# Attention with a top-score cut and a routed expert layer on one core: constant loads later and in fewer pieces, q's lower copy by GpSimd for pairs 2 to 9, and a new order table

## The chip, the cores and the metric

The kernel runs on one core of one Trainium2 chip. The metric is the device time of one execution in microseconds (us), lower is better. The core has TensorE (PE; PEld is its weight load), VectorE (DVE), ScalarE (ACT), GpSimd (POOL) and SyncE (SP), which here only issues transfers. Each engine works through its own instructions strictly in the order in which they stand in the program.

## The reference, cut to what matters

```python
# q, k, v: (8, 8, 576, 64) float32; tau = 0.02
scores = scale * np.matmul(q, k.transpose(0, 1, 3, 2))
thresh = np.max(scores, axis=-1, keepdims=True) - tau
scores = np.where(scores >= thresh, scores, -1000000000.0)
attn = softmax(scores)                       # over the last axis
x = heads joined of np.matmul(attn, v)       # (4608, 512)
# routed experts: 8 experts, 512 -> 1024 -> 512
logits = x @ w_gate + modality_bias[modality_id]
e_idx = np.argmax(logits, axis=1)            # one expert per token
out[token] = gate_w * (np.maximum(x @ w1[e], 0.0) @ w2[e])
```

## The kernel before

**Attention.** The 64 heads are taken in 32 pairs (4 pairs make a batch), and each pair in 9 steps of 128 query rows, 288 steps in all. A step is: scores on PE (`qk`, L819, into one of two PSUM tiles `s`), the row maximum on DVE (L828), a small addition on DVE (L830), the exponential on ACT (L834), the cut and the row sum on DVE (L846), four transposes on PE (L872), a copy on ACT (L875). The product with v (L753) follows by pairs in a tiling of PE of its own.

**Getting k and q ready.** fp32 accuracy is kept by splitting each value in a high and a low part (fp32r). For pairs 1 to 8, `load_rows` reads k and q into the single buffer `kq` in six pieces (two heads of k, two of q, one rest of each), `turn_rows` transposes it on PE (L684 a head, L690 the rests), `stack` makes the parts on POOL (L719, L721) in `q2`, k's in the lower 64 partitions and q's in the upper. Two transfers bring k's parts to `km`, and then one transfer, `move(q2[0:D], q2[D:P], 2.6)`, brings q's parts to the lower partitions too, over k's. `both_heads` builds `nk` and `qb` for the ninth step (L741 on POOL).

**Experts.** After each batch the tokens are routed (`gate`, `route`: small DVE operations, L1001 to L1034), and expert work on the tokens known so far (gathers, L1182 transposes, L1234 and L1266 matmuls) is laid between attention steps from about step 60 on. What is left runs after the attention.

**Constants.** `late_constants` loads the gate weights (`wgbd`), the modality bias and the modality numbers of all tokens (into an `xg` buffer, 8 bytes a token), computes `bias_t` on DVE, and fills the token table `tab` with one store. `bias_t` and `wgbd` are first used by the routing of batch 0.

**What sets the order.** Every operation is recorded with a due time (`at`, `tm`). `Plan.order` plays the operations through with fixed costs and takes, on each engine, the ready operation that is due first; `Plan.fill` puts matmuls on zeros (L1430) where PE would have a gap in that play. A table (`SHIFTS`) adds a small shift to due times before this. Nearly all transfers go out on SP's one queue, by `load` (L482), so a line says little and the tiles say much.

Of the kernel before, what the change touches and what calls it, by code (L numbers as in the profile page):

```python
# [341 lines left out]
def tile_attn_moe(  # L342
# [107 lines left out]
    RPOOL = 54  # L450

# [160 lines left out]
    def late_constants():  # L612
# [15 lines left out]
        mid_i = bi.t[:, 0:2 * B * NT].bitcast(I32).rearrange("p (b t two) -> p b t two", b=B, t=NT)  # L628
        mid_v = mid.bitcast(I32).rearrange("(b s two) -> b s two", s=S, two=2)
        for b in range(B):  # L630
            load(mid_i[:, b, 0:NC, :], mid_v[b, 0:SA, :].rearrange("(c p) two -> p c two", c=NC), wr=[(bi, b)], us=0.4)
        load(mid_i[:, :, NC, :], mid_v[:, S - P:S, :].rearrange("b p two -> p b two"), wr=[(bi, B)], us=0.7)
# [4 lines left out]
        def f():  # L637
            nc.vector.tensor_copy(out=mid_f[:, 1, :], in_=mid_i.rearrange("p b t two -> p (b t) two")[:, :, 0])
            nc.vector.tensor_scalar(out=mid_f[:, 0, :], in0=mid_f[:, 1, :], scalar1=0.0, scalar2=None,
                                    op0=ALU.is_equal)  # L640
        op("DVE", 0.25, f, [(bi, b) for b in range(B + 1)], [bf])
# [6 lines left out]
        for b, xs_ in ((bx, [bx]), (bi, [(bi, b) for b in range(B + 1)])):  # L648
            op("POOL", 0.45, lambda b=b: nc.gpsimd.memset(b.t, 0.0), wr=xs_ + [b])
# [19 lines left out]
    def load_rows(p):  # L669
# [3 lines left out]
        for z, src in enumerate((k, q)):  # L673
            for s in range(2):
                load(m[:, :, s, z, :], src[b, 2 * j + s, 0:SA, :].rearrange("(c p) d -> p c d", c=NC), us=0.6)
            load(rest(t)[:, :, z, :], src[b, 2 * j:2 * j + 2, SA:S, :].rearrange("s r d -> r s d"), us=0.2)
# [19 lines left out]
    def load_v(p):  # L696
        b, j = p // NPAIR, p % NPAIR
        t, r = vm2[p % 2], vr2[p % 2]
        sv = v[b, 2 * j:2 * j + 2]
        for s in range(2):  # L700
            load(t[:, s], sv[s, 0:SA, :].rearrange("(c p) d -> p c d", c=NC), us=0.6)
            load(r[s * R:(s + 1) * R], sv[:, SA:S, :].rearrange("s r d -> r s d"), us=0.2)
# [13 lines left out]
    def stack(p):  # L716
# [13 lines left out]
        for x in range(2):  # L730
            move(km[x * D:(x + 1) * D], q2[0:D, x], 1.3)
        move(q2[0:D], q2[D:P], 2.6)
# [91 lines left out]
    def soft_a(n):  # L824
# [5 lines left out]
        op("DVE", 0.21, lambda: nc.vector.tensor_scalar(out=nm[:, 1, x:x + 1], in0=nm[:, 0, x:x + 1], scalar1=-1.0,  # L830
                                                        scalar2=ntau, op0=ALU.mult, op1=ALU.add),
# [531 lines left out]
    at(30, late_constants)  # L1363
# [65 lines left out]
    def idle(g, n):  # L1429
# [3 lines left out]
    SHIFTS = [  # L1433
# [180 lines left out]
```

## Time and profile before

| | before |
|---|---|
| median of 3 runs | 1003.13 us (1002.33 to 1003.89) |
| profiled execution, its time | 999.88 us |
| its span, first to last instruction | 998.1 us |
| busy share PE, DVE, ACT, POOL | 97%, 74%, 62%, 56% |
| mean granted TensorE clock | 0.996 |

Busy shares are means over stages with different limits: attention alone at first, attention and experts from about 150 us, experts alone from about 785 us. The ends of matmuls are modelled, so a busy PE is not PE at its peak.

### The profile page before, as it was taken

To read this page: it belongs to the slowest core of one execution; us is meant where nothing else is said; L and a number is where in the kernel's file an instruction comes from. 1 tells how busy PE (TensorE), PEld (TensorE's weight loads), DVE (VectorE), ACT (ScalarE), POOL (GpSimd) and SP (SyncE) were. 2 spreads that over 40 slices of the span, in tenths; PEclk is the share of its full clock that TensorE was granted. 3 is DMA by queue.
4 is the path that set the end of the run, shared out by engine and by line. 5 is a ranking of instruction groups with operands and counts; after the bars stand their busy time and mean duration, and the time that the engine had idled before them with its cause. 6 is when DMAs were issued, how large, how long until landed. Compare 5 with 4: busy or idle time off the path is not lost.

```text
span 998.1 us, 20124 instructions
## 1 busy us (share of the span) xinstructions
PE 969.2 (97%) x6527; PEld 782.4 (78%) x6527; DVE 738.6 (74%) x1802; ACT 616.6 (62%) x1256; POOL 562.8 (56%) x693
## 2 busy tenths in 40 slices
PE   7989989999999999999999999999999999999997
PEld 6667678777888877888888778877887778888886
DVE  7889878898888888888988888878886373233341
ACT  6677667777777767777677667765775213243431
POOL 5433577475557652756666564646854679933341
PEclk9999999999999999999999999999999999999999
DMA  8787798789969975789689786987662258443421
GB/s 173 132 188 176 159 191 197 157 175 192 187 121 196 208 185 101 161 183 210 159 160 238 168 179 100 211 170 165 142 178 86 66 149 265 137 125 102 121 81 40
DMA packets 291122, 158.10 MB, mean 158 GB/s; under 512 B 199038, under 2 KB 262526, under 8 KB 289088
## 3 DMA queue, kind: packets, MB, share of 16 engines
q1 hardware_dynamic: 281696, 137.28, 63.0%
q0 software_dynamic: 7200, 18.92, 6.3%
q8 instruction: 54, 0.88, 0.4%
q10 hardware_dynamic: 2112, 0.52, 0.3%
q14 instruction: 60, 0.49, 0.2%
HBM read 85.83 MB, written 19.35 MB: 105 GB/s over the span
## 4 chain that ended last, share of the span: by engine, by line
PE 85%; DVE 5%; issue 3%; DMA 3%; ACT 1%; POOL 1%; SPq 0%; DVEq 0%; POOLq 0%; ACTq 0%
PE s L819 16%; PE bk L1266 16%; PE bk L753 15%; PE bk L1234 14%; PE bk L872 11%; PE pm L1234 3%; PE pm L1266 2%; PE bk L1182 1%; PE bk L941 1%; PE bk L885 1%; DMA tab<-pay,posi 1%; PE bk L966 1%; DVE nm L828 1%; DVE pr L846 1%; ACT e L834 1%
## 5 line engine op out<-in xcount | busy, mean ns | idle before, releaser
L828 DVE TENSOR_REDUCE nm<-s 128x1 f32<-128x576 f32 x288 | 216.4, 752 | 61.9 <-PE s L819 59.4
L834 ACT ACTIVATE e<-s,nm 128x576 f32<-128x576 f32 x288 | 213.5, 745 | 64.6 <-DVE nm L828 59.3
L846 DVE SCALAR_TENSOR_TENSOR pr<-s,nm,e 128x576 f32<-128x576 f32 x288 | 231.8, 812 | 25.7 <-ACT e L834 14.2
L819 PE MATMUL s<-km,q 128*128 128x288 f32 x1024 | 189.0, 310 | 2.9 <-DVE pr L846 2.7
L875 ACT COPY ptm<-bk 128x512 f32<-128x512 f32 x256 | 147.9, 588 | 57.8 <-PE bk L872 52.0
L819 PEld LDWEIGHTS s<-km,q 128*128 128x128 f32 x1024 | 146.9, 189 | 30.1 <-DVE pr L846 12.4
L872 PE MATMUL bk<-ident,pr 128*128 128x128 f32 x1152 | 168.8, 273 | 1.0 <-ACT kqt L687 1.0
L872 PEld LDWEIGHTS bk<-ident,pr 128*128 128x128 f32 x1152 | 137.3, 140 | 19.0 <-issue 3.3
L753 PE MATMUL bk<-ptm,v_m 128*64 128x320 f32 (+1 forms) x1024 | 137.8, 412 | 0.2
L753 PEld LDWEIGHTS bk<-ptm,v_m 128*64 128x64 f32 x1024 | 68.2, 136 | 48.8 <-issue 8.3
L1234 PE MATMUL bk<-xh,w1h 128*128 128x512 f32 (+2 forms) x244 | 92.6, 379 | 0.0
L1266 PE MATMUL bk<-w2h,hh 128*128 128x512 f32 x204 | 88.0, 431 | 3.0 <-DVE hl L1248 2.8
L721 POOL TENSOR_TENSOR q<-kqt,q 128x576 fp32r<-128x576 f32 x62 | 88.2, 1423 | 4.0
L1218 POOL TENSOR_TENSOR w1l<-raw,w1h 128x512 fp32r<-128x512 f32 x64 | 82.8, 1294 | 4.4
L1234 PE MATMUL bk<-xh,w1l 128*128 128x512 f32 (+2 forms) x244 | 85.2, 349 | 0.0
L1234 PE MATMUL bk<-xl,w1h 128*128 128x512 f32 (+2 forms) x244 | 85.1, 349 | 0.0
L1218 POOL TENSOR_TENSOR w2l<-raw,w2h 128x512 fp32r<-128x512 f32 x64 | 82.0, 1283 | 4.5
L719 POOL CAST q<-kqt 128x576 fp32r<-128x576 f32 x62 | 41.1, 665 | 72.7 <-PE s L819 54.9
L1266 PE MATMUL bk<-w2h,hl 128*128 128x512 f32 x204 | 80.9, 397 | 0.0
L1266 PE MATMUL bk<-w2l,hh 128*128 128x512 f32 x204 | 80.8, 396 | 0.0
L1216 POOL CAST w1h<-raw 128x512 fp32r<-128x512 f32 x64 | 39.6, 619 | 67.0 <-PE bk L1234 58.0
L1246 ACT ACTIVATE hh<-bk 128x512 fp32r<-128x512 f32 (+3 forms) x74 | 38.6, 521 | 58.8 <-PE bk L1234 58.1
(232 smaller groups left out, 1780.3 us busy)
## 6 DMA issues: line engine op xcount, KB each, us to landing
raw<-in_moe_w_dram SPq DMA_DIRECT2D x128, 256.0 KB, 4.0
km<-q SPq DMA_DIRECT2D x60, 288.0 KB, 4.4
q<-q SPq DMA_DIRECT2D x30, 576.0 KB, 5.1
nk<-km SPq DMA_DIRECT2D x97, 144.0 KB, 3.8
traw<-in_moe_w_dram SPq DMA_DIRECT2D x48, 256.0 KB, 3.0
v_m<-in_v_dram SPq DMA_DIRECT2D x64, 128.0 KB, 3.3
xs<-xr SPq DMA_DIRECT2D x32, 256.0 KB, 3.1
kq<-in_q_dram SPq DMA_DIRECT2D x46, 144.0 KB, 3.7
```

The lines of the kernel that those rows point to most:

```text
L719: op("POOL", 0.665, lambda s=s: nc.gpsimd.tensor_copy(out=q2[:, 0, s], in_=kqt[:, s]), [kqt[:, s]], [q2[:, 0, s]])
L721: op("POOL", 1.5, lambda s=s: nc.gpsimd.tensor_tensor(out=q2[:, 1, s], in0=kqt[:, s], in1=f32(q2[:, 0, s]), op=ALU.subtract), [kqt[:, s], ...
L753: nc.tensor.matmul(out=o, lhsT=lhsT, rhs=rhs, start=start, stop=stop, skip_group_check=True)
L819: nc.tensor.matmul(out=g.t[:, hf, 0:SH], lhsT=a, rhs=x, start=(z == 0), stop=(z == len(passes) - 1))
L828: op("DVE", 0.753, lambda: nc.vector.tensor_reduce(out=nm[:, 0, x:x + 1], in_=g.t[:, :, 0:SH], axis=AX.XY, op=ALU.max, negate=True), [g], ...
L834: op("ACT", 0.747, lambda: nc.scalar.activation(out=e, in_=g.t[:, :, 0:SH], func=AF.Exp, bias=nm[:, 0, x:x + 1]), [g, nm[:, 0, x:x + 1]], ...
L846: op("DVE", 0.88, lambda: nc.vector.scalar_tensor_tensor(out=pr.rearrange("p (a x) -> p a x", a=2), in0=g.t[:, :, 0:SH], scalar=nm[:, 1, x ...
L872: op("PE", 0.44, lambda: [nc.tensor.transpose(out=g.t[:, kc * P:(kc + 1) * P], in_=pr[:, kc * P:(kc + 1) * P], identity=ident) for kc in r ...
L875: op("ACT", 0.583, lambda: nc.scalar.copy(out=o, in_=g.t.rearrange("a (k p) -> a k p", p=P)), [g], [o])
L1218: op("DVE" if d else "POOL", 0.902 if d else 1.37, lambda: (nc.vector if d else nc.gpsimd).tensor_tensor(out=lo.t, in0=raw.t, in1=f32(hi.t ...
L1234: nc.tensor.matmul(out=g.t[:, 0:WT], lhsT=a.t[:, cs], rhs=x.t[:, c, 0:WT], start=(c == 0 and y == 0), stop=(c == KC - 1 and y == 2))
L1266: nc.tensor.matmul(out=g.t, lhsT=a.t[:, ts], rhs=w.t, start=(y == 0 and i == 0), stop=(y == F2 - 1 and i == 2))
```

## The change

- `late_constants` is due at 54 in place of 30, and the modality numbers come in two loads in place of nine; each load now moves 64 partitions by 72 or 71 elements of 8 bytes.
- `load_v` reads v of pairs 1 to 8 in one transfer for both heads, each partition four neighbouring rows, and `load_rows` reads k in the same order of rows, so that the keys of the scores and the rows of v still agree.
- For pairs 2 to 9 (`p < QPOOL`; pairs 0 and 1 go by heads) the last transfer of `stack` becomes two POOL copies.
- The table of shifts is replaced by one with a shift for every operation. (`NMPOOL` is 0, so L830 stays on DVE.)

```diff
+    QPOOL = 10
...
-        for b in range(B):
-            load(mid_i[:, b, 0:NC, :], mid_v[b, 0:SA, :].rearrange("(c p) two -> p c two", c=NC), wr=[(bi, b)], us=0.4)
-        load(mid_i[:, :, NC, :], mid_v[:, S - P:S, :].rearrange("b p two -> p b two"), wr=[(bi, B)], us=0.7)
+        NM = N // R
+        mid_i = bi.t[:, 0:2 * NM].bitcast(I32).rearrange("p (m two) -> p m two", two=2)
+        mid_v = mid.bitcast(I32).rearrange("(m r two) -> r m two", r=R, two=2)
+        for h in range(2):
+            load(mid_i[h * R:(h + 1) * R, 0:NM - h, :], mid_v[:, h:, :], wr=[(bi, h)], us=1.6)
...
-                load(m[:, :, s, z, :], src[b, 2 * j + s, 0:SA, :].rearrange("(c p) d -> p c d", c=NC), us=0.6)
+                kc = src[b, 2 * j + s, 0:SA, :]
+                load(m[:, :, s, z, :], kc.rearrange("(p c) d -> p c d", c=NC) if z == 0 else
+                     kc.rearrange("(c p) d -> p c d", c=NC), us=0.6)
...
+        if 0 < p < ROWS:
+            load(t.rearrange("p s c d -> p s (c d)"), sv[:, 0:SA, :].rearrange("s (p c) d -> p s (c d)", c=NC), us=1.2)
+        else:
+            for s in range(2):
+                load(t[:, s], sv[s, 0:SA, :].rearrange("(c p) d -> p c d", c=NC), us=0.6)
...
+        if p < QPOOL:
+            for s in range(2):
+                op("POOL", 1.33, lambda s=s: nc.gpsimd.tensor_copy(out=q2[0:D, :, s], in_=f32(q2[D:P, :, s])),
+                   [q2[D:P, :, s]], [q2[0:D, :, s]])
+            return
         move(q2[0:D], q2[D:P], 2.6)
...
-    at(30, late_constants)
+    at(54, late_constants)
...
-        (515427, 173, 233, 0.3), (614633, 760, 820, 3), (985271, 408, 558, 0.1), (531926, 381, 406, 0.3),
...
+        "PrPZREQHT-OWP<OiOQPYQTP4O~PIT8N|M=Q(Q'O{N>R5OKS~KMPqPSQ$PSPMPKPSP]P<PgPUPZPWPDPIPbPlPJP?PVT9LUS|NFPb"
...
+    for o, x, y in zip(plan.ops, SHIFTS[0::2], SHIFTS[1::2]):
+        o.due = o.due + (91 * digit[x] + digit[y] - 4140) / 100
```

The first place is SP's queue where the constants stand: the modality numbers and bias go to `xg`, the gate weights to `wgbd`, the fill to `tab`; the `kq` rows below them are the load of pair 4. Before:

```order
L482 DMA xg_100<-in_moe_modality_id_dram 128x4x2
L482 DMA wgbd<-in_moe_w_gate_dram 64x4x8
L482 DMA q_162<-q_162 64x2304
L482 DMA xg_100<-in_moe_modality_id_dram 128x4x2 x6
L482 DMA xg_99<-in_moe_modality_bias_dram 128x16
L482 DMA xg_100<-in_moe_modality_id_dram 128x4x2
L482 DMA tab<-xr_192 128x592
L482 DMA xg_100<-in_moe_modality_id_dram 128x8x2
L482 DMA wgbd<-in_moe_w_gate_dram 64x4x8
L482 DMA qb_167<-q_162 64x2x64
L482 DMA kq<-in_k_dram 64x2x64
L482 DMA kq<-in_q_dram 64x2x64
```

The same place now:

```order
L484 DMA qb_167<-q_162 64x2x64
L484 DMA xg_100<-in_moe_modality_id_dram 64x71x2
L484 DMA xg_100<-in_moe_modality_id_dram 64x72x2
L484 DMA wgbd<-in_moe_w_gate_dram 64x4x8
L484 DMA kq<-in_q_dram 128x4x64
L484 DMA kq<-in_k_dram 128x4x64
L484 DMA wgbd<-in_moe_w_gate_dram 64x4x8
L484 DMA xg_99<-in_moe_modality_bias_dram 128x16
L484 DMA kq<-in_k_dram 64x2x64
L484 DMA kq<-in_q_dram 128x4x64
L484 DMA kq<-in_k_dram 128x4x64
L484 DMA kq<-in_q_dram 64x2x64
```

Twelve issues for constants and the fill of `tab` stood ahead of pair 4's load; now three stand ahead of its first piece, two more between its pieces, and `tab` is filled 17 rows further on, between pieces of pair 5's load.

The second place is PE around the ends of pairs 4 and 5's transposes (`bk<-ident,kq` 128x128: a head of the single buffer `kq`). Before, at step 25; the first of the two transposes is pair 4's last, the second pair 5's first:

```order
L819 MATMUL s_76<-km_164,q_162 128x288 x4
L872 MATMUL bk_79<-ident,pr_180 128x128 x4
L872 MATMUL bk_78<-ident,pr_179 128x128 x4
L684 MATMUL bk_77<-ident,kq 128x128 x4
L684 MATMUL bk_80<-ident,kq 128x128 x4
L819 MATMUL s_75<-km_164,q_162 128x288 x4
L872 MATMUL bk_79<-ident,pr_181 128x128 x4
L819 MATMUL s_76<-nk,qb_167 128x288 x6
```

Now, with both heads of pair 5 behind the step on `nk` (step 26):

```order
L835 MATMUL s_75<-nk,qb_167 128x288 x6
L889 MATMUL bk_78<-ident,pr_178 128x128 x4
L769 MATMUL bk_77<-ptm_0_182,v_m_171 64x256 x4
L691 MATMUL bk_80<-ident,kq 128x128 x4
L691 MATMUL bk_79<-ident,kq 128x128 x4
L835 MATMUL s_76<-km_165,q_163 128x288 x4
L697 MATMUL bk_78<-ident,kq 128x64 x2
```

Pair 4's last transpose stands 18 rows above the first of these two, with five score steps between; before, nothing stood between them.

The third place is POOL where pair 2's copy comes in (`q_162` is its `q2`; `rp<-pr` is the small copy of each step). Before, the cast for `qb` waits for the transfer that fills the lower half:

```order
L859 COPY rp<-pr_179 128x64
L859 COPY rp<-pr_180 128x64
L741 CAST qb_167<-q_162 64x2x64
L719 CAST q_163<-kqt 128x576
L721 TENSOR_TENSOR q_163<-kqt,q_163 128x576
```

Now:

```order
L876 COPY rp<-pr_181 128x64
L745 CAST q_162<-q_162 64x2x576 x2
L757 CAST qb_167<-q_162 64x2x64
L876 COPY rp<-pr_178 128x64
L876 COPY rp<-pr_179 128x64
L730 CAST q_163<-kqt 128x576
L732 TENSOR_TENSOR q_163<-kqt,q_163 128x576
```

The two copies stand between small copies of two steps, and must wait until k's parts have been read from the half that they overwrite. In the rest of the program PE holds the same real matmuls; the matmuls on zeros that `fill` adds number 145 in place of 119, and the first transposes of gathered tokens stand behind step 58 in place of step 60.

## Rows read from the trace of the kernel before

**Rows 1.** Page, part 1: engine, busy us, share of the span, instructions.
```profile
PE 969.2 (97%) x6527; PEld 782.4 (78%) x6527; DVE 738.6 (74%) x1802; ACT 616.6 (62%) x1256; POOL 562.8 (56%) x693
```
**Rows 2.** Stretches of 25 us: length, busy by engine, clock, DMA share, GB/s.
```profile
core 0: us, PE busy (x) PEld busy (x) DVE busy (x) ACT busy (x) POOL busy (x), PEclk, DMA share, GB/s
25.00:50.00 25.00, 23.82 (x176) 17.23 (x177) 21.22 (x55) 17.11 (x31) 10.09 (x23) 1.00 0.70 132
50.00:75.00 25.00, 22.14 (x178) 17.45 (x179) 21.01 (x55) 17.65 (x33) 7.80 (x19) 1.00 0.82 189
75.00:100.00 25.00, 24.24 (x187) 17.74 (x187) 22.69 (x57) 19.16 (x35) 8.03 (x20) 1.00 0.78 174
100.00:125.00 25.00, 24.12 (x204) 17.16 (x203) 21.88 (x67) 15.77 (x30) 13.65 (x23) 1.00 0.75 160
125.00:150.00 25.00, 22.45 (x179) 18.14 (x176) 19.99 (x51) 17.27 (x36) 20.02 (x25) 1.00 0.92 191
```
**Rows 3.** Line L828, one instruction a step, in two of these stretches.
```profile
50.00:75.00 25.00, 8.26 (x11) 1.00 0.82 189
75.00:100.00 25.00, 9.23 (x13) 1.00 0.78 174
```
**Rows 4.** Waits of PE, whole span: who for whom, us, times, longest.
```profile
PE bk L684 <- DMA kq<-in_q_dram: 3.9, 3, 2.5
...
PE bk L753 <- DVE oh L1009: 2.8, 4, 1.3
...
PE bk L1182 <- DMA xg<-xs,tb: 2.2, 1, 2.2
```
**Rows 5.** Chain that ended last, 0 to 135 us: start, us, what.
```profile
47.45 2.08 DMA kq<-in_q_dram
...
49.97 0.83 PE bk L1430 x13
...
61.66 2.84 DMA kq<-in_q_dram
```
**Rows 6.** Timeline of PE: start, us; idle before and releaser in brackets.
```profile
49.66 0.30 PE L690 MATMUL bk<-ident,kq 64*128 64x64 f32 x2 [0.75 <-DMA kq<-in_q_dram]
...
64.59 0.63 PE L684 MATMUL bk<-ident,kq 128*128 128x128 f32 x4 [2.53 <-DMA kq<-in_q_dram]
```
**Rows 7.** Timeline of SP's queue near the constants.
```profile
37.81 5.10 SPq L482 DMA_DIRECT2D xg<-in_moe_modality_id_dram  x6
...
46.80 0.60 SPq L482 DMA_DIRECT2D kq<-in_k_dram  x1
```
**Rows 8.** DMA, 41 to 42 us: packets; queue, packets, MB, engine share.
```profile
DMA packets 1074, 0.01 MB, mean 8 GB/s; under 512 B 1074, under 2 KB 1074, under 8 KB 1074
...
q1 hardware_dynamic: 1074, 0.01, 59.9%
```
**Rows 9.** Page, part 6: transfers, count, KB each, median us to landing.
```profile
q<-q SPq DMA_DIRECT2D x30, 576.0 KB, 5.1
```
**Rows 10.** Timeline of POOL: the cast of 64 by 576 values.
```profile
45.11 0.66 POOL L741 CAST nk<-km 64x576 fp32r<-64x576 f32 x1 [0.37 <-PE s L819]
```
**Rows 11.** Timeline, 190 to 198 us: POOL and DVE.
```profile
194.56 1.43 POOL L721 TENSOR_TENSOR q<-kqt,q 128x576 fp32r<-128x576 f32 x1
194.57 1.48 DVE L1006 SCALAR_TENSOR_TENSOR fe<-l,iota_m 128x40 f32<-128x40 f32 x1
```
**Rows 12.** Lines of DVE to 125 us: busy, mean ns, idle before.
```profile
L846 DVE SCALAR_TENSOR_TENSOR pr<-s,nm,e 128x576 f32<-128x576 f32 x51 | 41.3, 814 | 4.2 <-ACT e L834 1.8 <-POOL q L721 0.6
```
**Rows 13.** The same, 125 to 800 us.
```profile
L846 DVE SCALAR_TENSOR_TENSOR pr<-s,nm,e 128x576 f32<-128x576 f32 x238 | 191.3, 812 | 21.5 <-ACT e L834 12.4 <-PE bk L872 2.6 <-DVE nm L830 0.5
```
**Rows 14.** Line L1006, one a batch: ns min/median/max, first and last start.
```profile
L1006 DVE SCALAR_TENSOR_TENSOR fe<-l,iota_m x8: 199/582/1476, 108.1 to 782.5; 128x40 f32<-128x40 f32 x8
```
**Rows 15.** Timeline of the start.
```profile
3.27 0.51 SPq L482 DMA_DIRECT2D raw<-in_q_dram  x1
...
3.99 0.62 SPq L482 DMA_DIRECT2D y<-in_q_dram  x1
...
7.40 1.33 PE L819 MATMUL s<-km,q 128*128 128x288 f32 x8
...
23.40 0.76 DVE L828 TENSOR_REDUCE nm<-s 128x1 f32<-128x576 f32 x1
```
**Rows 16.** Lines of PE, whole span: the matmuls on zeros.
```profile
L1430 PE MATMUL bk<-zero 128*128 128x128 bf16 x119 | 8.0, 219 | 0.0
```

More of the change, by code (lines that the diff above doesn't have):

```diff
@@ L450, in tile_attn_moe @@
     RPOOL = 54
+    NMPOOL = 0
+    QPOOL = 10
     def tm(n):
@@ L627, in late_constants @@
              us=0.2)
-        mid_i = bi.t[:, 0:2 * B * NT].bitcast(I32).rearrange("p (b t two) -> p b t two", b=B, t=NT)
-        mid_v = mid.bitcast(I32).rearrange("(b s two) -> b s two", s=S, two=2)
-        for b in range(B):
-            load(mid_i[:, b, 0:NC, :], mid_v[b, 0:SA, :].rearrange("(c p) two -> p c two", c=NC), wr=[(bi, b)], us=0.4)
-        load(mid_i[:, :, NC, :], mid_v[:, S - P:S, :].rearrange("b p two -> p b two"), wr=[(bi, B)], us=0.7)
+        NM = N // R
[3 more added lines that the diff above has]
+            load(mid_i[h * R:(h + 1) * R, 0:NM - h, :], mid_v[:, h:, :], wr=[(bi, h)], us=1.6)
+        mid_b = mid_i[:, :, 0].rearrange("p (b m) -> p b m", b=B)
         mid_f = bf.t[:, 0:2 * B * NT].rearrange("p (a x) -> p a x", a=2)
@@ L637, in f @@
         def f():
-            nc.vector.tensor_copy(out=mid_f[:, 1, :], in_=mid_i.rearrange("p b t two -> p (b t) two")[:, :, 0])
+            mid_t = mid_f[:, 1, :].rearrange("p (b t) -> p b t", b=B)
+            nc.vector.tensor_copy(out=mid_t[:, :, 0:NC], in_=mid_b[:, :, 0:2 * NC:2])
+            nc.vector.tensor_copy(out=mid_t[:, :, NC], in_=mid_b[:, :, 2 * NC - 1])
             nc.vector.tensor_scalar(out=mid_f[:, 0, :], in0=mid_f[:, 1, :], scalar1=0.0, scalar2=None,
                                     op0=ALU.is_equal)
-        op("DVE", 0.25, f, [(bi, b) for b in range(B + 1)], [bf])
+        op("DVE", 0.25, f, [(bi, 0), (bi, 1)], [bf])
         for m, (t, key) in enumerate(((bias_t, bias_t), (bias_u, bu))):
@@ L647, in late_constants @@
            [bias_t, bu], [bias_t])
-        for b, xs_ in ((bx, [bx]), (bi, [(bi, b) for b in range(B + 1)])):
+        for b, xs_ in ((bx, [bx]), (bi, [(bi, 0), (bi, 1)])):
             op("POOL", 0.45, lambda b=b: nc.gpsimd.memset(b.t, 0.0), wr=xs_ + [b])
@@ L699, in load_v @@
         sv = v[b, 2 * j:2 * j + 2]
+        if 0 < p < ROWS:
[3 more added lines that the diff above has]
+                load(t[:, s], sv[s, 0:SA, :].rearrange("(c p) d -> p c d", c=NC), us=0.6)
         for s in range(2):
-            load(t[:, s], sv[s, 0:SA, :].rearrange("(c p) d -> p c d", c=NC), us=0.6)
             load(r[s * R:(s + 1) * R], sv[:, SA:S, :].rearrange("s r d -> r s d"), us=0.2)
@@ L829, in soft_a @@
                                                          negate=True), [g], [nm[:, 0, x:x + 1]], hot=1)
-        op("DVE", 0.21, lambda: nc.vector.tensor_scalar(out=nm[:, 1, x:x + 1], in0=nm[:, 0, x:x + 1], scalar1=-1.0,
-                                                        scalar2=ntau, op0=ALU.mult, op1=ALU.add),
+        pool = n < NMPOOL
+        op("POOL" if pool else "DVE", 0.21, lambda: (nc.gpsimd if pool else nc.vector).tensor_scalar(
+            out=nm[:, 1, x:x + 1], in0=nm[:, 0, x:x + 1], scalar1=-1.0, scalar2=ntau, op0=ALU.mult, op1=ALU.add),
            [nm[:, 0, x:x + 1], ntau], [nm[:, 1, x:x + 1]], hot=1)
@@ L1562, in tile_attn_moe @@
+    digit = {c: i for i, c in enumerate(c for c in map(chr, range(35, 127)) if c != chr(92))}
+    assert len(SHIFTS) == 2 * len(plan.ops)
+    for o, x, y in zip(plan.ops, SHIFTS[0::2], SHIFTS[1::2]):
+        o.due = o.due + (91 * digit[x] + digit[y] - 4140) / 100
     with tc.manual_schedule():
```

123 lines of the change are left out of this document (115 added, 8 removed), and 119 rows, old and new, of the table SHIFTS.

## The prediction

> **What bounds the kernel now.** I began with the busy shares: PE is busy 969.2 of 998.1 us [rows 1], so about 29 us of PE's idle time, and what PE does for nothing, is all that a new order can win. The table of stretches shows where: the first 150 us. There PE is idle 1.2, 2.9, 0.8, 0.9 and 2.6 us in five stretches [rows 2], while only attention runs. In that stage DVE sets the pace. It is busy 21.2 and 21.0 of 25 us in the second and third stretch and 22.7 in the fourth [rows 2], and the fourth takes 13 steps where the third takes 11 [rows 3]. So the second and third stretch hold a stall that the fourth doesn't have. PE's waits name it: `kq<-in_q_dram`, 3.9 us in three waits [rows 4]. In the chain of waits two of these stand out, a transfer at 47.45 and one at 61.66 [rows 5], and the timeline gives what PE lost to them: 0.75 us before 49.66 and 2.53 us before 64.59 [rows 6]. From 150 us on, PE has little idle time; its larger waits there are 2.8 us for `oh` of the routing and 2.2 us for one gather [rows 4].
>
> **The wait before 49.66.** It is pair 4's rest of q. SP issued its load as late as 47.45, next after k's at 46.80, because SP had been issuing constants: six of the modality loads alone took 5.10 us from 37.81 on [rows 7]. Now five issues stand where eight modality loads and the rest did, and only three of them ahead of pair 4's first piece. At 0.85 us an issue (5.10 / 6) that is some 6 us of SP's time less, more than the 2 us that the load was late by. I take the 0.75 us as gone. Behind it, 13 matmuls on zeros took 0.83 us [rows 5], put there for a gap; `fill` no longer places any at this step, so they go too: 1.6 us together.
>
> **The wait before 64.59.** Here the constants have no part. Pair 5's first transposes stood straight behind pair 4's last in PE's order, but their load, into the same buffer, was issued at 61.66 and took 2.84 us [rows 5]. The new order puts five score steps between the two, about 10 us at 25 / 11 us a step [rows 3], against a load that needs some 3 to 4 us with its issue. The fill of `tab` stands among these loads now; one issue more. I take the 2.53 us as gone.
>
> **What they are worth.** 1.6 + 2.5 = 4.1 us on PE. But DVE must use them. If the second and third stretch ran at the fourth's DVE share, they would gain (22.69 - 21.22) + (22.69 - 21.01) = 3.15 us of DVE work [rows 2], which at that share is 3.15 x 25 / 22.69 = 3.5 us. I take **-3.5 us**, with 0 and -4.1 as bounds.
>
> **The start.** SP's first two loads were head 0's; now head 1's come first, and SP's halves of head 0 are fifth and sixth, issued about where 3.27 and 3.99 stand [rows 15]: 2 us later. The first scores, at 7.40 [rows 15], would come up to 2.1 us later. In exchange head 1 is made ready ahead of the steps and not between steps 2 and 4, and the same DVE work is done either way. Counting the new DVE order forward from a first maximum at about 10.4, with two steps in about 4.1 us, I get the eighth at about 23.4, where it stands before [rows 15]. I take **0**, with 0 and +2.1 as bounds.
>
> **Experts two steps earlier.** The stage without experts loses two steps. PE is idle 5.7 of 100 us from 25 to 125 us (1.18 + 2.86 + 0.76 + 0.88) [rows 2], and two steps take about 4.2 us: 4.2 x 0.057 = **-0.2 us**, bounds 0 and -0.5.
>
> **q's lower copy on POOL.** A cast of 64 by 576 values takes 0.66 us [rows 10]; each copy holds twice that, 1.3 us, and there are 16: 21 us more for POOL between about 35 and 210 us. No row shows a POOL copy that moves values to other partitions, so below the bound is this 21 us, and above it, at L721's 1.43 us for 576 values a partition [rows 11], 16 x 2.9 = 46 us. I take the first, since a cast is nearest. Cover: POOL is busy 8 to 14 of 25 us until 125 us and 20 in the next stretch [rows 2], and the result is wanted steps later. Behind a copy stand the small copies `rp`, whose source buffer DVE needs four steps on, some 8 us; without this cover a copy would cost DVE its 1.3 us, or 4 to 5 with the landing of `km` that it waits for. In exchange eight transfers of 576 KB, 5.1 us to landing [rows 9], go from a queue whose engines are 0.70 to 0.92 busy [rows 2]. The one later DMA wait of PE that they could shorten is the gather's 2.2 us [rows 4]. I take **0**, with +5 and -2.2 as bounds.
>
> A rule speaks against these copies. At 194.57 the routing's `fe`, which reads two SBUF operands, took 1.48 us while a two-operand POOL operation ran from 194.56 to 195.99 [rows 11]; the fastest `fe` takes 199 ns, the median 582 [rows 14]. The Trainium skill (SBUF — State Buffer, Who interferes with whom) says why: VectorE and GpSimd share a port pair that is locked for a whole instruction, and a VectorE instruction with two SBUF inputs waits for GpSimd's reads, one with a single SBUF input does not. By that rule, the trace agrees, the 288 long DVE operations, which read PSUM and at most one SBUF tensor, lose nothing: `pr` takes 814 ns where POOL is mostly idle and 812 where it is busy [rows 12, 13]. The routings of batches 0 and 1 fall among the copies. One hit each would be 2 x 1.3 = 2.6 us at most; in eight routings PE lost 2.8 us by `oh` [rows 4], 0.35 each. I leave it at 0, with +2.6 as bound.
>
> **v and k loads.** One v load for two, in longer runs: PE waits nowhere for v above, so 0. Where v was hidden it stays so.
>
> **The rest of the order.** 26 more matmuls on zeros at 8.0 / 119 = 0.067 us are 1.7 us [rows 16] where no gap is under them, and nothing where one is. The waits after 150 us are drawn anew: 2.2 + 2.8 us [rows 4] could go, as much could come. I take 0, with -5 and +5 as bounds.
>
> **Sum.** -3.5 + 0 - 0.2 + 0 + 0 = -3.7 us. The profiled execution's span of 998.1 becomes 994.4, its time of 999.88 becomes 996.2. It lies 3.25 us under the median of the runs, 1003.13, and the forecast is made for that median: 1003.13 - 3.7 = **999.4 us**.
>
> **Rivals.**
> *The stall only moves.* `kq` remains one buffer, and every pair's load waits for the transposes of the pair before; the new table may put another pair where pair 5 was. For it: three such waits stand in the early trace, at different pairs [rows 4]. Against it: at both known places the distance grew. Half the gain is lost and some fills cost: about 1002.5 us.
> *Slower: the modality packets block the loads behind them.* From 41 to 42 us 1074 packets of 8 bytes kept 59.9% of 16 engines busy [rows 8], so 16 x 0.599 us / 1074 = 8.9 ns each. The old nine loads had 8 x 512 + 1,024 = 5,120 of them, spread over 9 us; the two new ones have 64 x (72 + 71) = 9,152, next to each other: 9,152 x 8.9 ns / 16 = 5.1 us of the whole DMA, directly ahead of pair 4's load on the same queue. If that load lands 5.1 us later and PE stands at its first transpose, the old 1.6 us wait grows to 5.1 and pair 5 comes late in turn: 1003.13 + 5.1 - 1.6 = 1006.6 us. It decides as soon as the slack of pair 4's load is under 5 us; I count about 4 to 5 us between its landing and step 19, so it is near.
> *More than the stall.* The copies' DMA time and the new table also take away the gather's and `oh`'s waits: 999.4 - 4 = 995.4 us.
>
> **Chances.** Forecast 0.44 (996.5 to 1001 by itself), more 0.14, moved stall 0.20, blocked loads or another mishap of the start 0.22. A measurement of this kernel can tell about 0.2%, 2 us. So faster 0.58, same 0.20, slower 0.22. The range from 994.5 to 1005 holds all but the low half of the third rival and the high half of the second.
>
> **What would show it.** Right: no PE wait for `kq` over 1 us between 25 and 75 us; 12 or 13 steps in each of these stretches; DVE near 22.5 of 25 us there; POOL copies of 1.3 us with DVE never waiting for `rp`; first scores near 9.5 and the eighth maximum near 23.4. Wrong: a wait of 2 us or more for `kq` before step 30, or POOL copies of 2 us and more; new PE waits after 150 us of over 5 us in sum.

## The result, and the profile after

| | before | after |
|---|---|---|
| median of 4 runs | 1002.73 us (1001.81 to 1003.89) | 1012.05 us (1011.22 to 1013.00) |
| profiled execution, its span | 998.1 us | 1010.2 us |
| mean granted TensorE clock | 0.996 | 0.993 |

The changed kernel is **slower**: a ratio of 1.0086, 95% interval 1.0068 to 1.0104. 999.4 us was forecast, and the range ended at 1005.0.

The page's first part, against [rows 1]: engine, busy us, share, instructions.

```profile
PE 975.1 (97%) x6553; PEld 790.3 (78%) x6553; DVE 738.4 (73%) x1803; ACT 618.1 (61%) x1256; POOL 579.4 (57%) x709
```

PE does the same work but for 26 matmuls on zeros; yet it is busy 5.9 us longer and idle 6.2 us longer (1010.2 - 975.1 against 998.1 - 969.2). The stretches of 25 us, against [rows 2], show both:

```profile
core 0: us, PE busy (x) PEld busy (x) DVE busy (x) ACT busy (x) POOL busy (x), PEclk, DMA share, GB/s
25.00:50.00 25.00, 21.48 (x165) 16.39 (x162) 20.56 (x54) 16.95 (x30) 15.13 (x27) 1.00 0.77 125
50.00:75.00 25.00, 23.73 (x159) 17.16 (x159) 18.74 (x45) 15.00 (x27) 10.20 (x21) 0.87 0.59 140
75.00:100.00 25.00, 24.23 (x184) 18.30 (x183) 22.47 (x58) 19.33 (x35) 12.12 (x23) 1.00 0.59 141
100.00:125.00 25.00, 22.59 (x201) 17.02 (x200) 23.30 (x66) 16.40 (x31) 9.78 (x18) 1.00 0.50 112
125.00:150.00 25.00, 20.97 (x165) 16.12 (x163) 17.36 (x44) 13.86 (x27) 21.77 (x31) 0.93 0.66 158
```

Idle time alone misleads here. From 50 to 75 us PE is busier than before (23.73 against 22.14) with fewer matmuls (159 against 178): the clock was 0.87 in the mean, so 0.13 x 25 = 3.3 us of PE's time were lost to it. Idle time and lost clock together are 12.0 + 3.3 + 1.8 = 17.0 us from 25 to 150 us; before, at a clock of 1.00 throughout, they were 8.2 [rows 2]. That is 8.8 us, most of the loss. From 150 to 790 us PE is hardly idle, 5.2 and 1.4 us in two long stretches, so little is left there to make it good with (same columns).

```profile
150.00:450.00 300.00, 294.78 (x2147) 240.44 (x2146) 256.46 (x644) 218.21 (x460) 179.80 (x201) 1.00 0.78 166
450.00:790.00 340.00, 338.63 (x2415) 274.67 (x2414) 277.45 (x691) 235.07 (x498) 205.65 (x228) 1.00 0.73 165
```

The row maxima, one a step, show when the loss comes. Steps are counted from 0. Step 20 stood 8.3 us later than before (61.36 for 53.05), step 50 only 4.2, step 62 9.1, and the last one 10.9; in a second profile of the changed kernel (`after_again`) these were 7.9, 5.0, 6.2 and 13.4. So the new order makes good a part of a first delay by itself, and then loses again. DVE's timelines, steps 50 and 62, first before, then after:

```profile
122.79 0.75 DVE L828 TENSOR_REDUCE nm<-s 128x1 f32<-128x576 f32 x1
149.72 0.76 DVE L828 TENSOR_REDUCE nm<-s 128x1 f32<-128x576 f32 x1
```

```profile
127.00 0.76 DVE L844 TENSOR_REDUCE nm<-s 128x1 f32<-128x576 f32 x1
158.84 0.76 DVE L844 TENSOR_REDUCE nm<-s 128x1 f32<-128x576 f32 x1 [0.55 <-PE s L835]
```

PE's waits in the whole span, against [rows 4]:

```profile
PE s L835 <- DVE pr L863: 11.4, 16, 3.4
PE pm L1199 <- DVE xl L1204: 4.9, 1, 4.9
PE bk L769 <- DVE oh L1026: 2.7, 4, 1.2
PE bk L697 <- DMA kq<-in_q_dram: 1.9, 1, 1.9
```

Two places stand behind the two slow clocks. **The first, 37 to 54 us.** SP's timeline, against [rows 7] (start, us):

```profile
37.21 3.84 SPq L484 DMA_DIRECT2D xg<-in_moe_modality_id_dram  x2
41.09 2.76 SPq L484 DMA_DIRECT2D wgbd<-in_moe_w_gate_dram  x1
43.96 0.55 SPq L484 DMA_DIRECT2D kq<-in_q_dram  x1
...
48.71 0.62 SPq L484 DMA_DIRECT2D kq<-in_q_dram  x1
```

And PE's timeline, against [rows 6] (idle before and releaser in brackets):

```profile
47.85 1.07 PE L835 MATMUL s<-nk,qb 128*128 128x288 f32 x6 [1.57 <-DVE pr L863]
48.76 0.60 PE L889 MATMUL bk<-ident,pr 128*128 128x128 f32 x4
51.27 0.44 PE L697 MATMUL bk<-ident,kq 64*128 64x64 f32 x2 [1.91 <-DMA kq<-in_q_dram]
51.64 1.33 PE L835 MATMUL s<-km,q 128*128 128x288 f32 x4
52.76 1.05 PE L889 MATMUL bk<-ident,pr 128*128 128x128 f32 x4
```

Three issues took 6.6 us. Two things came late by it. DVE stood 1.25 us for the modality numbers, and its `pr` behind that released PE's first wait:

```profile
45.31 0.19 DVE L642 CAST y<-xg 128x32 f32<-128x32 int32 x1 [1.25 <-DMA xg<-in_moe_modality_id_dram]
```

And pair 4's rest of q went out at 48.71 (before at 47.45 [rows 5]), which was PE's second wait. It is the last of the load's six pieces now; before, the rests were the first two. Behind the waits the same four transposes took 1.05 us instead of 0.60: PE had fallen from the upper clock level (2.4 GHz) to the lower (1.2 GHz). The granted clock was 0.50 from 51.0 to 56.5 us.

**The second, 118 to 134 us.** POOL's timeline:

```profile
118.07 0.98 POOL L1055 DMA_INDIRECT tab<-pay,posi  x1 [0.30 <-issue]
119.04 0.42 POOL L876 COPY rp<-pr 128x64 f32<-128x64 f32 x2
126.54 1.15 POOL L745 CAST q<-q 64x1152 fp32r<-64x1152 f32 x1 [7.08 <-DMA tab<-pay,posi]
...
130.84 0.58 POOL L876 COPY rp<-pr 128x64 f32<-128x64 f32 x3
```

DVE's and PE's timelines there:

```profile
131.46 0.82 DVE L863 SCALAR_TENSOR_TENSOR pr<-s,nm,e 128x576 f32<-128x576 f32 x1 [3.45 <-POOL rp L876]
...
132.34 1.33 PE L835 MATMUL s<-km,q 128*128 128x288 f32 x4 [3.40 <-DVE pr L863]
133.46 1.05 PE L889 MATMUL bk<-ident,pr 128*128 128x128 f32 x4
```

Pair 6's copy of q stood 7.08 us, not for k's transfers but for the scatters of the routing, which POOL had issued just before. Behind it stood two more scatters, a cast and the small copies `rp`; DVE needed their source buffer, PE needed DVE, and then the clock fell. In the built program the copy's waits say the same (`DMASW` 1 to 3 belong to the three scatters ahead of it, `DMAHW` 4 and 7 to the two transfers of k's parts, which had been issued at 112.22 and 114.50):

```
L876 COPY rp<-pr_181 128x64
L745 CAST q_162<-q_162 64x2x576 [waits DMASW3_49,DMAHW4_49,DMASW2_49,DMAHW7_49,DMASW1_49,Pool_49]
L1055 DMA tab<-pay,posi_204 37888x2 [waits Pool_49]
```

In `after_again` the copy stood 5.84 us, but DVE only 1.06, and the clock was 1.00 from 100 to 150 us. What this place costs differs between executions.

### The profile page after: what moved, and what is told of

It reads as the page before. It is cut to its first block, busy times and chain, and to the rows that moved or that the text cites. A ratio compares the mean times of both kernels' runs of the same rounds, so it can differ in the third digit from the quotient of the medians.

```text
span 1010.2 us, 20147 instructions
## 1 busy us (share of the span) xinstructions
PE 975.1 (97%) x6553; PEld 790.3 (78%) x6553; DVE 738.4 (73%) x1803; ACT 618.1 (61%) x1256; POOL 579.4 (57%) x709
## 4 chain that ended last, share of the span: by engine, by line
PE 82%; DVE 9%; issue 3%; DMA 3%; POOL 1%; ACT 1%; SPq 1%; POOLq 0%; DVEq 0%; ACTq 0%
PE s L835 16%; PE bk L1251 16%; PE bk L769 14%; PE bk L1283 14%; PE bk L889 10%; PE pm L1283 3%; PE pm L1251 2%; DVE pr L863 2%; DVE nm L844 2%; DMA tab<-pay,posi 1%; PE bk L902 1%; PE bk L958 1%; PE bk L1199 1%; PE bk L983 1%; DVE fe L1023 1%
## 5 line engine op out<-in xcount | busy, mean ns | idle before, releaser
L835 PE MATMUL s<-km,q 128*128 128x288 f32 x1024 | 191.1, 313 | 10.2 <-DVE pr L863 9.1
L769 PE MATMUL bk<-ptm,v_m 128*64 128x256 f32 (+1 forms) x1024 | 138.2, 413 | 0.8 <-ACT ptm L895 0.8
L1265 DVE SCALAR_TENSOR_TENSOR hl<-bk,hh 128x512 fp32r<-128x512 f32 (+3 forms) x78 | 46.2, 594 | 55.9 <-ACT hh L1263 55.7
L1283 PE MATMUL bk<-w2h,hh 128*128 128x512 f32 x196 | 84.1, 429 | 0.0
L1263 ACT ACTIVATE hh<-bk 128x512 fp32r<-128x512 f32 (+3 forms) x78 | 41.1, 527 | 60.2 <-PE bk L1251 59.4
L1283 PE MATMUL bk<-w2h,hl 128*128 128x512 f32 x196 | 77.5, 395 | 0.0
L1283 PE MATMUL bk<-w2l,hh 128*128 128x512 f32 x196 | 77.4, 395 | 0.0
```

The source lines that it names most:

```text
L769: nc.tensor.matmul(out=o, lhsT=lhsT, rhs=rhs, start=start, stop=stop, skip_group_check=True)
L835: nc.tensor.matmul(out=g.t[:, hf, 0:SH], lhsT=a, rhs=x, start=(z == 0), stop=(z == len(passes) - 1))
L1265: op("DVE", 0.1 + 0.58 * WT / 512, lambda: nc.vector.scalar_tensor_tensor(out=hl.t[:, 0:WT], in0=g.t[:, 0:WT], scalar=0.0, in1=f32(hh.t[:, ...
L1283: nc.tensor.matmul(out=g.t, lhsT=a.t[:, ts], rhs=w.t, start=(y == 0 and i == 0), stop=(y == F2 - 1 and i == 2))
```

## The experiments

Each ratio is to runs of the kernel before on the same chip; 0.001 is about 1 us. The runs lie on several chips, and the changed kernel itself measured 1.0086 on one and 1.0128 on another, so small differences between two ratios are not read as gains. **Theory A** at first: the loss lies at three places, the late first scores and the two above. **Rival B**: the GpSimd copies cost something at every pair. **Rival C**: the order as such.

**1. The transfer back, for all eight pairs and for two.**

```diff
-                op("POOL", 1.33, lambda s=s: nc.gpsimd.tensor_copy(out=q2[0:D, :, s], in_=f32(q2[D:P, :, s])),
+                op("POOL", 1.33, lambda s=s: nc.sync.dma_start(out=f32(q2[0:D]), in_=f32(q2[D:P])) if s else None,
```

In the second kernel this holds for `p in (6, 7)` only.

> The changed kernel in its own order, but q's lower copy of pairs 2 to 9 is again one transfer on SP, issued where the second GpSimd copy stood. Theory A (the loss lies at three places: first scores 4.3 us later, 45 to 62 us, and 119 to 132 us, where a GpSimd copy stands 7.1 us before the scatters' landing and the small copies rp behind it hold the row maxima): only the third goes, 3 to 5 us of it, so 1007 to 1009 us, and no wait of DVE for rp over 1 us is left. Rival B (the copies cost something at each of the eight pairs, by GpSimd's queue or by a port shared with DVE): 6 us or more go, 1006 us or less. Rival C (the order alone, the copies cost nothing): 1011 to 1013 us.

> The changed kernel, with the transfer back for pairs 6 and 7 alone, whose copies stand behind scatters or gathers on GpSimd's queue; the other twelve copies stay on GpSimd. Theory A: as much as with all eight pairs undone, 3 to 5 us, so 1007 to 1009 us. Rival B: only a quarter of what all eight pairs give, 1 to 2 us, so 1010 to 1011 us. Rival C: 1011 to 1013 us.

Measured: 1.0111 (1.0081 to 1.0140) and 1.0081 (1.0056 to 1.0107). Rival B is not borne out: without the copies this order is no faster. With all eight transfers back, pair 2's stands on SP among the pieces of pair 4's load, and PE's wait for pair 4's rest of q grows from 1.9 to 3.7 us. Theory A isn't borne out either: undoing the copies of pairs 6 and 7, the second place, gave nothing that can be measured here, although in its profile DVE's wait for `rp` is gone and the clock is 1.00 from 75 to 150 us.

**2. Fewer packets for the modality numbers.** First in longer runs:

```diff
-        mid_v = mid.bitcast(I32).rearrange("(m r two) -> r m two", r=R, two=2)
+        mid_w = mid.bitcast(I32).rearrange("(r m two) -> r m two", r=R, two=2)
```

> The changed kernel, but the two loads of the modality numbers read 72 neighbouring tokens for a partition (about 130 packets instead of 9,152; the same two issues and the same bytes). Each token gets another token's number, so the biases of the gate are dealt out otherwise. Theory A with the packets as the cause of the second place (k's and q's rests lie behind them in the queue): DVE's wait for them at 45 us and PE's wait for q's rest at 51 us (1.9 us) go, 1 to 3.5 us, so 1008.5 to 1011 us. Rival (the second place is the order of the issues on SP, the packets are hidden): 1011.5 to 1012.5 us.

Then in one load of 71 runs, turned by PE:

```diff
+            g = fin["spare"]()
+            nc.tensor.transpose(out=g[:, 0:71], in_=bi.t[0:71, 256:384], identity=ident[0:71, 0:71])
```

> The changed kernel in its own order, but the modality numbers come in one load of 71 runs of 1 KB (71 packets instead of 9,152), issued where the first of the two loads stood, and are turned by one transpose on PE where DVE turned them into floating point. The output is the reference's, so the routing is as in the changed kernel. Theory A (the packets hold up k's and q's rests behind them, which stops the steps at 45 to 62 us): at step 20 the row maximum stands at most 4 us behind before instead of 8.3, and 3 to 5 us of the loss of 8.6 go: a ratio to before of 1.0035 to 1.0055. Rival (the run with long runs gained in its tail by its other routing): 0 to 2 us, a ratio of 1.0065 to 1.009.

Measured: 1.0027 (1.0001 to 1.0054) and 1.0095 (1.0067 to 1.0124). The first was a false trail: it leaves out the right numbers, so its experts get other tokens and its work behind the attention isn't the same. Whether that made its time is not shown: its last row maximum stood at 772.2 us and its span ended at 1001.4, with the reference's routing in `a_pe_numbers` these were 774.4 and 1011.4, but in `after_again`, with the reference's routing too, 777.5 and 1006.1. In the second run the first place is mended in part. SP's timeline:

```profile
37.86 0.72 SPq L634 DMA_DIRECT2D xg<-in_moe_modality_id_dram  x1
38.63 0.64 SPq L484 DMA_DIRECT2D wgbd<-in_moe_w_gate_dram  x1
...
44.69 0.61 SPq L484 DMA_DIRECT2D kq<-in_q_dram  x1
```

PE's wait for the rest of q is gone and step 20's row maximum stands at 58.2 us in place of 61.4 (before 53.1), 5.1 us late where theory A wanted at most 4. Still the time did not follow, and the steps show where the gain went: at step 50 0.2 us of its 3.2 are left (126.83 for 127.00). The packets by themselves aren't the loss.

**3. The parts in the order of before.** `b_two_loads` has the two modality loads alone, `b_pool_copies` the copies alone, `b_parts` all three parts, `b_pool_pe` the copies and the numbers by PE. The copies, at the transfer's place in the order:

```diff
-        move(q2[0:D], q2[D:P], 2.6)
+        def copy():
+            for s in range(2):
+                nc.gpsimd.tensor_copy(out=q2[0:D, :, s], in_=f32(q2[D:P, :, s]))
+        op("SP", 0.62, copy if p < 10 else lambda: nc.sync.dma_start(out=f32(q2[0:D]), in_=f32(q2[D:P])),
+           [q2[D:P]], [q2[0:D]], dma=2.6)
```

> The kernel before in its own order; only the transfer of q's parts for pairs 2 to 9 is replaced, at its place in the order, by two GpSimd copies. In this order the copies of pair 6 stand ahead of the scatters and one pair's stand behind scatters and gathers. Theory A (a copy costs only where it stands behind indirect transfers or a late transfer of k): within 2 us of before, 1001 to 1005 us. Rival B (a cost at every pair, some 0.5 us or more each): 1007 us or more. A gain from q being ready earlier: below 1001 us.

> The kernel before in its own order; only its nine loads of the modality numbers (5,120 packets) are replaced by the changed kernel's two (9,152 packets), issued at the place of the second and third of the nine. Packets as the cause (4,032 more at 8.9 ns over 16 queues, 2.2 us, ahead of pair 4's load): 1 to 4 us slower, a ratio of 1.001 to 1.004, and PE's wait for pair 4's rest of q at 49.7 us grows. Rival (seven issues fewer on SP, some 4 us, let pair 4's load start earlier and outweigh the packets): a ratio of 0.997 to 0.9995.

> All three parts of the change (two loads of the numbers, one load of v and k in the new order of rows for pairs 1 to 8, GpSimd's copies for pairs 2 to 9), but in the order of the kernel before: what stays away is the new order and the later constants. If the parts lose: a ratio of 1.004 or more. If the new order loses and the parts give what the copies alone gave (0.997): 0.995 to 1.001.

> The kernel before in its own order, with GpSimd's copies for pairs 2 to 9 (alone a ratio of 0.997) and the modality numbers in one load of 71 packets with a transpose on PE instead of nine loads of 5,120 packets. If packets ahead of pair 4's load are what delays the steps at 45 to 52 us in this order too: the wait before 49.7 us goes and the ratio is 0.993 to 0.996. If they are hidden here: 0.996 to 0.998, as with the copies alone.

| | ratio | 95% |
|---|---|---|
| b_pool_copies | 0.9970 | 0.9952 to 0.9989 |
| b_two_loads | 0.9998 | 0.9977 to 1.0019 |
| b_parts | 0.9988 | 0.9971 to 1.0005 |
| b_pool_pe | 0.9955 | 0.9935 to 0.9975 |

So the parts lose nothing where the order is that of before; the copies win about 3 us (1 to 5). In `b_pool_pe` DVE is busy as the prediction wanted it from 50 to 75 us (against 21.01 before); so it is in `b_pool_copies` and `b_parts` (22.61 each), without the new order. `b_pool_copies` and `b_pool_pe` beat both kernels; which of the two is faster is not shown. `b_pool_pe`:

```profile
50.00:75.00 25.00, 23.31 (x180) 17.80 (x179) 22.57 (x59) 18.21 (x35) 10.73 (x22) 1.00 0.64 149
```

Rival C stands: what loses is the new order, the later constants with it. **Theory D**: it loses in the first 150 us, where PE's idle time and clock say so. **Rival E**: later.

**4. Where the order loses.** The changed kernel with all its parts, its operations laid out by a written list, two orders spliced at a step: one order up to that step's row maximum, the other order for all that is left.

```diff
-        for i in plan.fill(plan.order(4, marks["close"]), 4, idle):
-            o = plan.ops[i]
+        plan.order(4, marks["close"])
+        ROW = (
...
+        for x in ROW.split():
+            i, *bk = x.split(":")
...
+            o = plan.ops[int(i)]
```

> The changed kernel, unaltered, beside the three orders of the same call: a ratio to before of 1.0068 to 1.0104, as measured first.

> The changed kernel with all its parts; the order of the kernel before up to the row maximum of step 62 (some 150 us), and from there its own. Theory D (the order loses, and it loses in the first 150 us: there PE's idle time and the time lost to the lower clock together rise from 13.7 to 22 us, later they hardly differ): a ratio of 0.997 to 1.002. Rival E (the new order loses later, between steps, gathers and experts): 1.006 or more.

> The reverse: the changed kernel with its own order up to step 62, and from there the order of the kernel before. Theory D: the loss stays, a ratio of 1.006 to 1.010. Rival E: 0.997 to 1.003.

> The changed kernel with the order of the kernel before up to step 20 only (some 53 us: the first loads, the constants and pair 4's load lie in it), then its own. Theory D: the start and the place at 45 to 62 us are mended, the one at 119 to 132 us (4.7 us of PE's idle and clock by the windows) stays: a ratio of 1.003 to 1.006. If the first 53 us hold the whole loss: 0.997 to 1.002. Rival E: 1.006 or more.

> The changed kernel with the order of the kernel before up to step 8 only (some 26 us: the first loads and scores), then its own. If the late first scores cost what they show (4.3 us at the first row maximum, 3 at the eighth): 3 us less than the changed kernel, a ratio of 1.005 to 1.008. If PE makes good use of the wait (its idle time in the first 25 us is no longer than before, 4.9 against 5.4 us) and the place at 45 us decides: no gain, a ratio of 1.009 to 1.013.

> The changed kernel with the order of the kernel before up to step 40 (some 96 us). With the same up to step 20 the ratio was 1.0069, up to step 62 it was 1.0009. If what is left after step 20 is the place at 119 to 132 us: 1.005 to 1.008, as up to step 20. If it is lost between 53 and 96 us: 1.000 to 1.003.

> The changed kernel's parts with its own order up to step 20 only (some 53 us), and the order of the kernel before from there. All of the parts in the order of before had a ratio of 0.9988, all in the new order 1.0086 and 1.0128. If the first 53 us of the new order cost what taking them away gave (about half): 1.003 to 1.007. If the rest of before's order makes good for them: 0.997 to 1.002.

| | order to the step | from there | ratio | 95% |
|---|---|---|---|---|
| after_again | after | after | 1.0128 | 1.0091 to 1.0164 |
| o_a62_b | after, 62 | before | 1.0122 | 1.0077 to 1.0167 |
| o_b8_a | before, 8 | after | 1.0087 | 1.0058 to 1.0116 |
| o_b20_a | before, 20 | after | 1.0069 | 1.0046 to 1.0093 |
| o_b40_a | before, 40 | after | 1.0060 | 1.0038 to 1.0082 |
| o_b62_a | before, 62 | after | 1.0009 | 0.9991 to 1.0028 |
| o_a20_b | after, 20 | before | 1.0057 | 1.0035 to 1.0079 |

Theory D holds from both sides: with the first 62 steps in the order of before the loss is gone, with only these in the new order it is all there. Steps 0 to 20 in the new order cost 1.0057 - 0.9988 = 0.69% (0.4 to 1.0), 7 us. Steps 20 to 40 cost nothing that can be told, steps 40 to 62 cost 1.0060 - 1.0009 = 0.5% (0.2 to 0.8), 5 us. Taken away, steps 0 to 20 gave less: from 1.0086 and 1.0128 to 1.0069, 0.2 to 0.6%. The profiles agree: behind a new start the order of before leaves step 50 9.2 us late (`o_a20_b`), the new order only 4.2. The start alone (`o_b8_a`) gives nothing clear back.

**5. The copy behind the scatters, by itself.** Once taken away where the first 20 steps are mended, by the edit of experiment 1, and once put into the order of before, as here against `b_pool_copies` (long lines shortened):

```diff
             sent.append(i)
+            if len(sent) == 3:
+                held.pop()()
...
-        op("SP", 0.62, copy if p < 10 else
+        op("SP", 0.62, (lambda: held.append(copy)) if p == 6 else copy if p < 10 else
```

> As o_b20_a (order of the kernel before up to step 20, a ratio of 1.0069), and q's parts of pairs 6 and 7 by a transfer instead of GpSimd's copies, which there stand behind scatters and gathers. If DVE's wait for rp behind these copies (3.5 us) and the clock behind it are what is left: 4 to 6 us less, a ratio of 1.000 to 1.004. If it only moves (the transfer is as late): 1.005 to 1.009.

> The kernel before in its own order with GpSimd's copies for pairs 2 to 9 (alone a ratio of 0.997), and one thing moved: pair 6's two copies are issued right behind the third scatter, as in the changed kernel, where they wait for the three scatters' landing. If this wait alone costs what it shows in the changed kernel (GpSimd idle some 7 us, DVE waiting 1 to 6 us for rp, then half clock): 3 to 7 us more than with the copies in their old place, a ratio of 1.000 to 1.004. If it is harmless in this order: 0.995 to 0.999.

Taken away: 1.0049 (1.0024 to 1.0074) against 1.0069, which is no clear gain. In its profile the clock is 1.00 up to 150 us and step 62 comes where it came before (149.65), but step 80 5.2 us later (206.96 for 201.75): the delay has moved behind step 62. Put in: 1.0028 (1.0011 to 1.0044) against 0.9970, so **in the order of before this one move costs 0.58% (0.3 to 0.8), 6 us**, and its profile has the same waits as the changed kernel's. POOL's timeline, then DVE's:

```profile
111.68 0.98 POOL L1045 DMA_INDIRECT tab<-pay,posi  x1 [0.32 <-issue]
122.03 2.23 POOL L737 CAST q<-q 64x1152 fp32r<-64x1152 f32 x2 [9.37 <-DMA tab<-pay,posi]
```

```profile
124.59 0.82 DVE L853 SCALAR_TENSOR_TENSOR pr<-s,nm,e 128x576 f32<-128x576 f32 x1 [5.72 <-POOL rp L866]
```

In `b_pool_copies` the same two copies stand ahead of the scatters and wait for nothing:

```profile
108.16 2.24 POOL L734 CAST q<-q 64x1152 fp32r<-64x1152 f32 x2
...
111.66 1.07 POOL L1042 DMA_INDIRECT tab<-pay,posi  x1 [1.25 <-issue]
```

**6. Matmuls on zeros in the waits of the first place**, 20 before the scores of step 17 and 26 before the transpose of pair 4's rests:

```diff
+            if i[0] == "z":
+                g = Group()
+                g.t = banks[int(bk[0])]
+                idle(g, int(i[1:]))()
+                continue
```

> The changed kernel with 20 zero matmuls before the scores of step 17 and 26 before the transpose of pair 4's rests, the two places where PE waits 1.6 and 1.9 us at 47.9 and 51.3 us and works at half clock behind them. If the lower clock is what makes these waits dear (3 to 5 us by the windows of 0 to 100 us): 3 to 5 us less, a ratio of 1.005 to 1.009, and a granted clock of 1.00 from 25 to 100 us. If only the waits count: no gain, 1.009 to 1.013.

Measured: 1.0089 (1.0056 to 1.0121). The clock did stay up:

```profile
50.00:75.00 25.00, 24.07 (x194) 17.63 (x193) 19.74 (x50) 16.88 (x30) 11.14 (x24) 1.00 0.66 158
```

But the time did not move by what can be measured. Step 20 came 1.7 us earlier than in the changed kernel, and in this profile the copy behind the scatters then waited 9.7 us in place of 7.1, DVE 6.1 in place of 3.5: a gain at the first place can be given back at the second, where all wait for a landing. Step 62 came 2.7 us later than in the changed kernel (161.5 for 158.8).

## Why the prediction was wrong, point by point

- **"The rest of the order ... I take 0, with -5 and +5 as bounds."** This is the term that failed. The order before step 62 is all of the loss that can be measured: some 7 us up to step 20 and some 5 us from 40 to 62, each placed by splicing, where the bound was 5 in all. The second part is the stretch in which the copy stands behind the scatters and has the size that this move costs in the order of before, so it is likely the next point's loss and not another; that is argued, since taking the copy away in the new order gave nothing clear back. The prediction read the two waits that the new order removes and the waits of the old profile after 150 us; it did not follow what the new order puts behind what up to 150 us.
- **q's copies, "0, with +5 and -2.2 as bounds".** The cover was that `rp` is wanted some 8 us later, and the price without it "4 to 5 with the landing of `km`". Wrong landing: the copy waits for the scatters ahead of it on POOL, 5.8 to 10.9 us in the profiles of the changed kernel and the splices that keep this place. (In three of these, `o_b8_a`, `o_b20_a` and `o_a62_b`, the profile names a load of `raw` as the last to land; in the built programs of all three the copy waits for the scatters and k's transfers alone.) The bound was nearly right (6 us measured in `b_copies_late`); the zero was not. The copies' length was right (1.15 us each for 1.3), and so, nearly, was the bound of the gain: ahead of the scatters, the copies win 3 us.
- **"I take the 0.75 us as gone"** (the wait before 49.66). It became 1.91 us, and two steps failed. One is "at 0.85 us an issue": that was a mean of six, five at 0.5 to 0.6 us and one of 2.21, and now the second modality issue took 3.00 us and the small `wgbd` load behind it 2.76. The other is that issues ahead of pair 4's first piece were counted, while PE waits for the rest of q, which the new order moved from the second piece to the sixth. The tile `xg` on SP's queue (ns min/median/max), first before, then after:

```profile
L482 SPq DMA_DIRECT2D xg<-in_moe_modality_id_dram x6: 492/536/2215, 37.8 to 42.4; - x6
```

```profile
L484 SPq DMA_DIRECT2D xg<-in_moe_modality_id_dram x2: 793/1896/3000, 37.2 to 38.0; - x2
```

  The rival "the modality packets block the loads behind them" named the mechanism, and it showed (from 36.5 to 44 us 9,074 packets of its queue kept 89.1% of the engines busy); its price was wrong, since the packets gone gave nothing measurable, and in the order of before (`b_two_loads`) they cost nothing that can be measured.
- **The wait before 64.59** went, as forecast: pair 4's last head is transposed at 63.94 (before at 61.46), and pair 5's heads, at 74.09 in place of 64.59, wait for nothing:

```profile
74.09 1.09 PE L691 MATMUL bk<-ident,kq 128*128 128x128 f32 x8
```

  "12 or 13 steps in each of these stretches" did not come: 11 and 9. The 3.5 us of gain were eaten ahead of it.
- **The start, 0.** The first maximum stood at 12.58 for a forecast of 10.4, the eighth at 26.45 for 23.4, both past the bound of 2.1; in time it isn't seen (`o_b8_a`). PE's idle time in the first 25 us was no longer than before. But three of the nine profiles with the new start have a granted clock of 0.93 there (`after_again`, `a_q_transfer`, `o_a62_b`), and none of those with the old start, so 0 is not shown either.
- **The port rule.** Right as weighed. Line by line for DVE up to 125 us, and the routing's `fe`, against [rows 12, 14]:

```profile
L863 DVE SCALAR_TENSOR_TENSOR pr<-s,nm,e 128x576 f32<-128x576 f32 x48 | 38.6, 812 | 3.4 <-ACT e L851 1.2 <-issue 0.3
```

```profile
L1023 DVE SCALAR_TENSOR_TENSOR fe<-l,iota_m x8: 200/917/1477, 111.2 to 793.8; 128x40 f32<-128x40 f32 x8
```

  `pr` takes 812 ns with copies on POOL, as without (814), and a single `fe` takes at most 1477 ns. The median `fe` rose from 582 to 917 ns, but PE's wait for `oh` stayed at 2.7 us (2.8 before). The Trainium skill (SBUF — State Buffer, Who interferes with whom) exempts VectorE instructions with at most one SBUF input, outside their two-port modes; by that rule, the trace agrees.
- **v and k loads, 0:** nothing contradicts it; all parts together are at 0.9988.
- **After 150 us, nothing:** right within the noise (`o_b62_a` 1.0009, `b_parts` 0.9988). The 4.9 us wait in the tail (L1199 for `xl`) is no sure loss of the change: `o_b20_a` and `o_b62_a`, which end in the new order, have 5.6 there, `after_again` has none, and the orders that end as before wait for `hl` instead, 2.8 us in the kernel before and 5.6 in `b_parts`.

What stays open: which of the waits up to step 20 makes the 7 us, and how much of the 5 us behind step 40 is the copy's. The start, the packets and the clock were each taken away alone, and none gave more than the measurement's uncertainty; together, by the order of before, they gave 0.2 to 0.6%. Why the built program has the copy wait for the scatters was not settled.

## What to carry to other kernels

When an operation moves to another engine's queue, read in the built program what it waits for there, and what then stands behind it: a copy of 1.15 us became a wait of 7. Judge a new order by PE's idle time and its lost clock together, stretch by stretch, and then by when the steps come: in `a_pe_numbers` and `o_b20_a_q67` a mended wait only came back as a delay some steps later. When issues ahead of a load are counted, count up to the piece that is wanted first. And splicing two orders at a few steps places a loss that single edits don't.

## What the runs showed of the hardware

- An issue on SP is not a constant, and a load of some 4,600 packets of 8 bytes shows in the issue behind it: in the changed kernel the first of the two took 0.79 us, the second, behind it, 3.00, and the 8 KB load behind that 2.76. In `b_two_loads`, where other loads stand between, the two took 0.75 and 0.60 us and the small loads right behind them 2.81 and 4.37. One load of 71 packets of 1 KB took 0.72, and the load behind it 0.64.
- From an indirect scatter's issue at 118.07 to its landing passed 8.2 us (the copy released by it started at 126.54), and in `b_copies_late` some 10.
- A GpSimd copy of 64 by 1152 values to other partitions takes 1.15 us, less than two casts of 64 by 576 at 0.66 [rows 10].
- After waits of 1.57 and 1.91 us PE worked at the lower clock level for some 5 us: four scores of 128x288 took 1.33 us at 51.64 and 0.81 at 57.08. The one wait of 2.53 us in the kernel before [rows 6] had no such fall behind it: the clock was 1.00 in that stretch [rows 2].
